# The first projection of two token blocks by seven quarter products, with sums kept in PSUM

## The chip, the cores and the metric

The kernel runs on one core of one Trainium2 chip. The core has TensorE (PE in the profile; its weight loads are shown apart as PEld), VectorE (DVE), ScalarE (ACT), GpSimd (POOL) and SyncE (SP), which issues most of the DMAs. The metric is the device time of one execution in microseconds (us). Three runs of the kernel before gave 297.3, 298.53 and 298.81 us; the median, 298.53 us, is the time before.

## The reference

```python
def _attn_ref(q, k, v):                      # 8 batches, 8 heads, 576 positions, 64 wide
    scores = scale * np.matmul(q, k.transpose(0, 1, 3, 2))
    gamma = 1.0 - 2.0 ** (-5.0 - np.arange(H, dtype=np.float32))
    Dmat = np.where(rel >= 0, gamma[:, None, None] ** rel[None, :, :], 0.0)
    return np.matmul(scores * Dmat[None, :, :, :], v)
...
def _moe_ref(x, w_in, w_out, alpha):         # x: 4608 x 512, w_in: 512 x 2048, w_out: 2048 x 512
    h = x @ w_in
    s = np.sin(alpha * h)
    g = h + s * s / (alpha + 1e-09)
    return (g @ w_out).astype(np.float32)
```

The output of the attention (a decayed, causal one without softmax) is the `x` of the second function. The first projection is `x @ w_in`, the second `g @ w_out`.

## The kernel before, in words

The 4608 tokens are worked on in nine blocks of 512. Blocks 0 to 7 are the first 512 positions of batches 0 to 7; block 8 holds the last 64 positions of all eight batches. A block goes through four steps.

1. **Attention** leaves the block's `x` transposed and in float16 (`xT`, `xS` for block 8): model dimension on the partitions, in four slices, tokens along the free dimension.
2. **First projection.** The 2048 columns of `w_in` are cut into 16 chunks of 128, numbered `fc`. `project n fc` makes one chunk of block n by four matmuls (one for each slice of the model dimension) that add up 128x512 float32 values in one bank of PSUM (`hps`, L1745).
3. **The activation.** For each chunk `sine` (ScalarE, L1753) reads the PSUM bank and writes `s`, `square` (mostly ScalarE, L1762) writes `ss`, and `product` (VectorE, L1769) reads `ss` and the bank and writes the chunk of `gT` in float16. With that the bank is free.
4. **Second projection.** For blocks 3 to 8 it is done by seven products of quarters in place of eight (the Strassen scheme in Winograd's form): the block's 512x2048 matrix `g` and the 2048x512 `w_out` are each cut into 2 x 2 quarters. `row_sum` (VectorE, L1832) makes the four sums S1 to S4 of quarters of `g`, half of each at a time; `weight_sum` made the sums T1 to T4 of `w_out` once. `part_product n i` (L1849) is product i, 16 matmuls of 256 columns, and `after_product` adds what it gives to kept results in SBUF (`low`, `mid`) or to an output tile `osb`, which a DMA then stores.

The eight banks of PSUM have fixed names: `m0` and `m1` are two banks each, `h0`, `h1`, `h2` and `op` one each. A step takes the bank that its line names, and waits until the bank's last reader is done. Each engine works through its own instructions in one fixed order; an instruction that waits holds up everything behind it on its engine.

That order is written out by hand: the string `TABLE` has one line for each step, and `run` issues the steps from top to bottom, so that the order of lines is the order on every engine. `A`, `V` and `G` in a line choose ScalarE, VectorE or GpSimd. The steps that the change and the prediction touch are `project`, `sine`, `square`, `product`, `row_sum`, `part_product` and `after_product`.

Of the kernel before, what the change touches and what calls it, by code (L numbers as in the profile page):

```python
# [929 lines left out]
at.to_state 7 2  # L930
at.masked 7 0 0 @ret0
sine 6 4 @s0
square 6 4 A @ss0
product 6 4
project 6 11 h2
square 6 2 A @ss3
product 6 2
# [2 lines left out]
project 6 5 h0  # L940
sine 6 5 @s2
square 6 5 A @ss1
at.scores 7 1 0 m0
at.scores 7 1 1 m1
# [1 line left out]
at.masked 7 1 0 @ret1
project 6 7 h1
part_product 5 6 op
load 7 k 2
cast 6 k 2 G  # L950
sine 6 7 @s2
# [31 lines left out]
part_product 5 5 op
after_product 5 5
at.values 7 0 False m0 relay=G
square 6 9 A @ss0
load 7 q 2
at.more 7 3 @s320
project 6 14 h2
sine 6 14 @s3  # L990
product 6 9
part_product 5 3 - first=5
product 6 10
square 6 14 A @ss2
product 6 14
sine 6 12 @s0
square 6 12 A @ss2
at.values 7 1 False m1 relay=G
after_product 5 3
at.values 7 0 True  # L1000
at.add_states 7 0
# [21 lines left out]
square 6 15 A @ss2
square 7 0 A @ss3
project 7 1 m0
project 7 3 h1
cast 4 q 2 G
cast 6 v 2 G
product 6 15
sine 7 1 @s3  # L1030
square 7 1 A @ss1
part_product 6 1 op
after_product 6 1
product 7 0
product 7 1
sine 7 3 @s0
square 7 3 A @ss3
row_sum 6 S2 1 V
project 7 2 h0
sine 7 2 @s3  # L1040
ends.scores 0 m0
ends.masked 0
crossed 4 2 q
# [987 lines left out]
```

## Time and profile before

| | before |
|---|---|
| median of three runs | 298.53 us |
| the profiled execution's own time | 297.56 us |
| its span, first to last instruction | 295.8 us |
| PE busy | 284.9 us, 96% of the span |
| DVE busy | 223.8 us, 76% |
| ACT busy | 218.1 us, 74% |
| POOL busy | 141.0 us, 48%; one instruction in the last 65 us |
| TensorE clock granted | 1.0 throughout |

The profiled execution took 297.56 us, 1.76 us more than its span and 0.97 us less than the median of the runs. Busy time of an engine is the union of its instructions' records. Records of neighbouring instructions on one engine overlap a little, so the time from one start to the next is the better price where instructions follow each other directly, and the record is the better price where another engine waits for the result.

### The profile page before, as it was taken

To read this page: it belongs to the slowest core of one execution; us is meant where nothing else is said; L and a number is where in the kernel's file an instruction comes from. 1 tells how busy PE (TensorE), PEld (TensorE's weight loads), DVE (VectorE), ACT (ScalarE), POOL (GpSimd) and SP (SyncE) were. 2 spreads that over 40 slices of the span, in tenths; PEclk is the share of its full clock that TensorE was granted. 3 is DMA by queue.
4 is the path that set the end of the run, shared out by engine and by line. 5 is a ranking of instruction groups with operands and counts; after the bars stand their busy time and mean duration, and the time that the engine had idled before them with its cause. 6 is when DMAs were issued, how large, how long until landed. Compare 5 with 4: busy or idle time off the path is not lost.

```text
span 295.8 us, 8407 instructions
## 1 busy us (share of the span) xinstructions
PE 284.9 (96%) x3480; PEld 182.6 (62%) x3480; DVE 223.8 (76%) x316; ACT 218.1 (74%) x361; POOL 141.0 (48%) x151
## 2 busy tenths in 40 slices
PE   6789999999999999999999999999999999999993
PEld 4566545555545544455666666666776677676883
DVE  2596977788349776889988798869868785877863
ACT  2578935997595897977878896798679878888500
POOL 5684678565688685736439933956232000000000
PEclk9999999999999999999999999999999999999999
DMA  7999999998998999978899985984423101200124
GB/s 216 347 234 210 243 282 320 253 256 217 244 225 184 174 164 229 250 148 204 164 239 163 251 180 145 232 151 120 88 77 104 38 2 38 73 15 23 53 73 124
DMA packets 121767, 49.95 MB, mean 169 GB/s; under 512 B 78721, under 2 KB 119681, under 8 KB 121729
## 3 DMA queue, kind: packets, MB, share of 16 engines
q1 hardware_dynamic: 117920, 44.78, 63.5%
q0 software_dynamic: 2688, 4.19, 7.8%
q8 instruction: 27, 0.44, 0.6%
q10 hardware_dynamic: 1120, 0.44, 0.6%
q14 instruction: 12, 0.09, 0.1%
HBM read 36.75 MB, written 9.44 MB: 156 GB/s over the span
## 4 chain that ended last, share of the span: by engine, by line
PE 82%; DMA 9%; DVE 3%; ACT 2%; POOL 1%; SPq 1%; issue 1%; ACTq 0%; POOLq 0%
PE hps L1745 40%; PE hps L1849 23%; PE ops L1785 12%; DMA raw<-in_v_dram 3%; DMA w_in<-in_moe_w_in_dram 3%; PE o L1606 3%; PE sc L1564 2%; DMA raw<-in_k_dram 2%; DVE S L1832 1%; PE kv L1506 1%; DVE gT L1769 1%; PE o L1628 1%; SPq L1350 1%; POOL k L1396 1%; ACT s L1753 1%
## 5 line engine op out<-in xcount | busy, mean ns | idle before, releaser
L1769 DVE SCALAR_TENSOR_TENSOR gT<-ss,inva,hps 128x512 f16<-128x512 f16 x144 | 103.7, 743 | 36.0 <-ACT ss L1762 32.5
L1745 PE MATMUL hps<-xT,w_in 128*128 128x512 f16 (+1 forms) x532 | 120.2, 372 | 0.6 <-DMA w_in<-in_moe_w_in_dram 0.6
L1753 ACT ACTIVATE s<-hps,alpha_t 128x512 f16<-128x512 f32 x144 | 96.1, 683 | 30.4 <-PE hps L1745 29.5
L1745 PEld LDWEIGHTS <-w_in 128*128 128x128 f16 x596 | 65.6, 114 | 51.4 <-DMA w_in<-in_moe_w_in_dram 0.9
L1762 ACT ACTIVATE ss<-s 128x512 f16<-128x512 f16 x125 | 76.9, 629 | 5.9 <-DVE gT L1769 3.3
L1785 PE MATMUL ops<-w_out,gT 128*128 128x512 f16 x192 | 46.0, 380 | 0.0
L1849 PEld LDWEIGHTS <-gT 128*128 128x128 f16 x384 | 37.3, 98 | 7.5
L1396 POOL TENSOR_TENSOR k<-raw,cn 128x1024 f16<-128x1024 f32 (+1 forms) x17 | 29.5, 1736 | 20.9 <-DMA raw<-in_k_dram 18.4
L1849 PEld LDWEIGHTS <-S 128*128 128x128 f16 x288 | 28.1, 98 | 6.1
L1785 PEld LDWEIGHTS <-gT 128*128 128x128 f16 x192 | 17.9, 98 | 20.3
L1396 POOL TENSOR_TENSOR q<-raw,cn 128x1024 f16<-128x1024 f32 x13 | 25.1, 1937 | 3.7 <-PE o L1606 2.4
L1849 PE MATMUL hps<-T,gT 128*128 128x256 f16 x192 | 22.8, 273 | 0.0
L1849 PE MATMUL hps<-w_out,S 128*128 128x256 f16 x192 | 22.8, 273 | 0.0
L1849 PE MATMUL hps<-w_out,gT 128*128 128x256 f16 x192 | 22.8, 273 | 0.0
L1551 POOL TENSOR_TENSOR s<-kvs,cn 128x256 f32<-128x256 f32 x21 | 13.8, 659 | 16.3 <-ACT kvs L1320 8.8
L1322 POOL CAST v<-raw 128x1024 f16<-128x1024 f32 x10 | 10.3, 1037 | 21.8 <-DMA raw<-in_v_dram 20.0
L1576 DVE TENSOR_TENSOR ret<-sc,mask 128x1024 f16<-128x1024 f32 x16 | 19.2, 1219 | 1.6 <-PE sc L1564 1.6
L1552 POOL TENSOR_TENSOR kvs<-s,kvs 128x256 f32<-128x256 f32 x21 | 17.5, 833 | 3.9 <-DVE kvs L1322 1.2
L1576 DVE TENSOR_TENSOR ret<-sc,mask_halved 128x768 f16<-128x768 f32 x16 | 15.1, 954 | 3.7 <-PE sc L1564 3.6
L1320 ACT CAST xT<-o 128x1024 f16<-128x1024 f32 (+1 forms) x15 | 16.2, 1122 | 1.9 <-PE o L1628 1.9
L1832 DVE TENSOR_TENSOR S<-gT,S 128x1024 f16<-128x1024 f16 x24 | 17.4, 730 | 0.1
L1745 PE MATMUL hps<-xS,w_in 128*128 128x512 f16 x64 | 14.8, 379 | 0.0
(78 smaller groups left out, 265.6 us busy)
## 6 DMA issues: line engine op xcount, KB each, us to landing
raw<-in_q_dram SPq DMA_DIRECT2D x16, 512.0 KB, 5.3
out_dram<-osb SPq DMA_DIRECT2D x32, 256.0 KB, 2.9
raw<-in_k_dram SPq DMA_DIRECT2D x8, 512.0 KB, 6.1
raw<-in_v_dram SPq DMA_DIRECT2D x8, 512.0 KB, 6.3
raw<-in_v_dram SPq DMA_DIRECT2D x32, 128.0 KB, 3.5
raw<-in_k_dram SPq DMA_DIRECT2D x32, 128.0 KB, 3.7
w_in<-in_moe_w_in_dram POOLq DMA_DIRECT2D x4, 512.0 KB, 11.9
w_out<-in_moe_w_out_dram POOLq DMA_DIRECT2D x4, 512.0 KB, 13.2
```

The source lines that it names most:

```text
L1320: eng.copy(d_, s_)
L1396: eng.tensor_tensor(dst[:, a0:a1].rearrange("p a r t d -> p t (a r) d"), t_.rearrange("p (t a) x -> p t a x", t=2)[:, :, a0:a1].rearrange( ...
L1551: nc.gpsimd.tensor_tensor(s32, self.kvs[:, c - 1], g1.unsqueeze(2).to_broadcast([P, 4, D]), MULT)
L1552: nc.gpsimd.tensor_tensor(self.kvs[:, c], s32, self.kvs[:, c], ADD)
L1576: nc.vector.tensor_tensor(ret.rearrange("p t (z x) -> p (t z) x", z=2)[:, :, 0:n], sc.rearrange("p t (z x) -> p (t z) x", z=2)[:, :, 0:n], ...
L1745: matmul(hps_of[n, fc][0][:, cols], w_in16[fc // 4][:, a, fc % 4 :: 4], xs[n][:, a, cols], start=(a == 0 and part != 1), stop=(a == KT - 1 ...
L1753: nc.scalar.activation(s_t, hps, mybir.ActivationFunctionType.Sin, bias=0.0, scale=alpha_t[:, fc : fc + 1],)
L1762: nc.scalar.activation(ss_t, s_t, mybir.ActivationFunctionType.Square)
L1769: nc.vector.scalar_tensor_tensor(gT[n][:, fc, :], ss_t, inva[:, fc : fc + 1], hps, MULT, ADD)
L1785: matmul(ops[n, c, cols.start][:, cols], gT[n][:, fk, c * P : (c + 1) * P], w_out16[:, fk, cols], start=(fk == 0), stop=(fk == FC - 1), sk ...
L1832: made = eng.tensor_tensor(out_, x, y, op)
L1849: matmul(acc[:, 256 * j : 256 * j + 256], lhs[:, x, 128 * j : 128 * j + 128], rhs[:, x], start=(tag is not None and j == js[0] and p == 0 ...
```

## The change

Blocks 7 and 8 now make their first projection by the seven-product scheme as well. Its left factor is `w_in` transposed, its right factor `xT`, and the quarters are halves of the model dimension by halves of the 2048 columns or of the 512 tokens.

- **Sums of the weights, once:** `in_sum` makes S1 to S4 of `w_in` in 16 instructions of 128x512 float16, 13 on GpSimd and 3 on VectorE. **Sums of x, for each of the two blocks:** four instructions `x_sum` of the same size, 4 on VectorE and 4 on GpSimd in all.
- **Pairs.** A pair u gives two chunks, and there are eight pairs to a block. Its four quarter results c11, c12, c21 and c22 and product 5 are 256 columns each; c11, product 5 and c12 lie in a two-bank buffer (`wide`, in `m0` or `m1`) and c21 and c22 in one bank (`narrow`, in `h0` or `h1`). Each product is two matmuls of 256 columns. The steps of a pair are, in the order that their data force: `pair` (products 1 and 5); `pair_copy` (c11 from PSUM to c21 in PSUM, ScalarE or VectorE) and `pair_keep` (product 5 to SBUF); `pair_6` (TensorE adds product 6 onto c21); `pair_add` (VectorE: c12 = c21 + product 5); `pair_7` (adds product 7 onto c21); `pair_end` (VectorE: c22 = c21 + product 5); `pair_3` onto c12, `pair_2` onto c11, and `pair_4` onto c21. Then one sine, one square and one product read the two halves in `wide`, and one of each read `narrow`. So `m0` with `h0` serves one pair at a time, `m1` with `h1` the next.
- **Where other work runs.** All lines of `TABLE` from the `square` of chunk 13 of block 5 on are written in a new order. From there on, 19 of the 32 `row_sum` steps are on GpSimd (before: none), eight of the 50 squares leave ScalarE (six to VectorE, two to GpSimd), two casts and one eviction change engine, two `to_state` steps go from GpSimd to VectorE. Steps before that line, the loads, and the number of second-projection products stay.

```diff
-project 8 2 h1
-project 8 1 h0
-sine 8 1 @s0
-square 8 1 A @ss1
-row_sum 7 S3 1 V
...
+pair 8 3 m0 h0
+part_product 7 2 - first=1
+sine 8 3 @s3
+pair_copy 8 3 A
+pair_keep 8 3 A @e1
+pair_6 8 3
+pair_add 8 3
+pair 8 2 m1 h1
+square 8 3 A @ss1
+product 8 3
+pair_copy 8 2 V
+pair_3 8 3
+pair_2 8 3
+sine 8 5 @s2
+row_sum 7 S2 1 G
+pair_7 8 3
+pair_end 8 3
+pair_6 8 2
+square 8 5 V @ss1
+pair_4 8 3
+pair_keep 8 2 A @e0
+sine 8 7 @s3
+square 8 7 G @ss2
+pair_add 8 2
+pair_7 8 2
+product 8 5
...
+    def in_product(n, u, i, dst, first=False):
+        g, x = divmod(u, 2)
+        left, right = FACTORS[i]
+        left = "S3" if i == 7 else left
+        lhs = in_piece(left, g)[..., x] if isinstance(left, str) else w_in_quarter(g, *left)[..., x]
+        rhs = x_piece(n, right) if isinstance(right, str) else x_quarter(n, *right)
+        for a in range(2):
+            matmul(
+                dst, lhs[:, a], rhs[:, a], start=(first and a == 0), stop=(a == 1), skip_group_check=True,
+            )
+
+    def pair(n, u, tag2, tag1):
...
+        both = psum.tile([P, 2, 512], F32, tag=tag2, bufs=1, name="wide")
+        one = psum.tile([P, 512], F32, tag=tag1, bufs=1, name="narrow")
+        pairs[n, u] = both[:, 0, 0:256], both[:, 0, 256:512], both[:, 1, 0:256], one[:, 0:256], one[:, 256:512]
...
+        in_product(n, u, 1, pairs[n, u][0], first=True)
+        in_product(n, u, 5, pairs[n, u][1])
+
+    def pair_copy(n, u, eng):
+        c11, p5, c12, c21, c22 = pairs[n, u]
+        copy(eng, c21, c11)
+
+    def pair_keep(n, u, eng):
...
+        copy(eng, kept_5[n, u], p5)
+
+    def pair_6(n, u):
+        in_product(n, u, 6, pairs[n, u][3])
+
+    def pair_add(n, u):
+        c11, p5, c12, c21, c22 = pairs[n, u]
+        nc.vector.tensor_tensor(c12, c21, kept_5[n, u], ADD)
+
+    def pair_7(n, u):
+        in_product(n, u, 7, pairs[n, u][3])
+
+    def pair_end(n, u):
+        c11, p5, c12, c21, c22 = pairs[n, u]
+        nc.vector.tensor_tensor(c22, c21, kept_5[n, u], ADD)
```

The order of instructions shows what this does to an engine. First VectorE in the first projection of block 8, in the kernel before. `gT<-ss,inva,hps` is `product`, `S..<-gT` and `gT<-gT` are `row_sum`, `mid` and `low` are `after_product`; numbers tell buffers apart.

```order
L1769 SCALAR_TENSOR_TENSOR gT_4598<-ss1_539,inva_69,hps_4612 128x512
L1769 SCALAR_TENSOR_TENSOR gT_4598<-ss3_563,inva_69,hps_4607 128x512
L1769 SCALAR_TENSOR_TENSOR gT_4598<-ss3_563,inva_69,hps_4651 128x512
L1769 SCALAR_TENSOR_TENSOR gT_4598<-ss1_539,inva_69,hps_4624 128x512
L1832 TENSOR_TENSOR gT_4598<-gT_4598 128x4x256
L1880 TENSOR_TENSOR mid_4695<-hps_4656,low_4673 128x512
```

Now the same engine in the same place of the changed kernel, from the `pair_add` of pair 8 1 to that of pair 8 3 (`wide_4700` with `narrow_4701` is pair 8 0, `wide_4735` with `narrow_4736` pair 8 1, the 478x buffers pair 8 3; `e0` and `e1` are kept products 5; L2021 is `pair_add`, L2028 `pair_end`, L1474 a copy, L1919 a square, L1924 `product`).

```order
L2021 TENSOR_TENSOR wide_4735<-narrow_4736,e1_4288 128x256
L2028 TENSOR_TENSOR narrow_4701<-narrow_4701,e0_4356 128x256
L2028 TENSOR_TENSOR narrow_4736<-narrow_4736,e1_4288 128x256
L1924 SCALAR_TENSOR_TENSOR gT_4699<-ss1_539,inva_69,wide_4700 128x512
L1919 TENSOR_TENSOR ss0_525<-s1_523 128x512
L1924 SCALAR_TENSOR_TENSOR gT_4699<-ss0_525,inva_69,narrow_4701 128x512
L1924 SCALAR_TENSOR_TENSOR gT_4699<-ss3_563,inva_69,wide_4735 128x512
L2163 TENSOR_TENSOR osb_4778<-hps_4591,mid_4491 128x512
L2021 TENSOR_TENSOR wide_4783<-narrow_4784,e1_4288 128x256
```

Between two products of a pair there now stand two adds, a square and an `after_product`, each of which waits for another engine.

GpSimd had one instruction left in this part of the kernel before (`sS<-kvs,cn`, the state of block 7). In the changed one it has these in the first projection of block 8 (`S..<-gT` and `gT<-gT` are `row_sum`, `in_T` is `x_sum`, `ss..<-s..` a square):

```order
L1978 TENSOR_TENSOR in_T3_4407<-in_T3_4407,xS_76 128x512
L1978 TENSOR_TENSOR in_T4_4730<-xS_76,in_T3_4407 128x512
L2100 TENSOR_TENSOR S2_0_2491<-gT_4278 128x1024
L2100 TENSOR_TENSOR gT_4278<-gT_4278 128x4x256
L2100 TENSOR_TENSOR S2_1_2582<-gT_4278 128x1024
L1919 TENSOR_TENSOR ss2_541<-s3_550 128x512
L1919 TENSOR_TENSOR ss1_539<-s0_517 128x512
L2100 TENSOR_TENSOR gT_4699<-gT_4699 128x4x256
```

Sums of the second projection that VectorE made before are behind each other on GpSimd, and two squares of block 8 are queued between them.

More of the change, by code (lines that the diff above doesn't have):

```diff
@@ L930 @@
[L930 to L937, printed above, removed]
+at.evict_bank 7 1 V
+part_product 4 4 h1
+row_sum 5 S1 0 V
+project 5 15 m0
+project 6 0 op
+sine 5 15 @s3
+square 5 15 A @ss3
+project 6 4 h0
+project 6 5 m1
+load 5 v 2
+after_product 4 4
+row_sum 5 S4 0 V
+sine 6 0 @s3
+product 5 15
+cast 4 v 2 A
+at.more 7 1 @s320
+square 6 0 V @ss3
+crossed 7 0 q @qT2
+at.more 7 2 @s320
+product 5 13
+part_product 5 1 h1
+project 6 2 h2
@@ L938 @@
+square 6 6 A @ss2
+project 6 8 h1
+sine 6 8 @s2
+square 6 8 A @ss0
+part_product 5 7 - first=6
+at.values 7 0 True
+at.add_states 7 0
+crossed 6 2 k
+product 6 7
+at.keep 7 0 A @xT0
+at.masked 7 1 0 @ret1
+product 6 6
+at.scores 7 1 1 m1
+project 6 10 h0
+sine 6 10 @s1
 load 6 v 2
 load 7 v 2
[L940 to L944, printed above, removed]
-at.masked 7 1 1 @ret3
[L946 to L951, printed above, removed]
@@ L983 @@
[L983 to L992, printed above, removed]
-product 6 10
[L994 to L1001, printed above, removed]
+cast 6 q 2 G
+product 6 8
+cast 6 v 2 A
+project 6 14 h1
+cast 4 q 2 G
+at.masked 7 1 1 @ret3
+in_sum S1 0 V
+crossed 4 2 q
+square 6 10 A @ss3
@@ L1023 @@
[L1023 to L1043, printed above, removed]
+product 6 14
+in_sum S2 1 G
+project 6 15 op
+project 6 13 h0
+project 6 9 h2
+ends.values 0 False m0
+crossed 6 2 q
+x_sum 7 T3 V
+x_sum 7 T1 V
 ends.scores 2 m1
@@ new lines @@
+product 7 1
+pair_copy 7 0 A
+in_sum S4 1 G
+pair_keep 7 0 A @e0
+pair_6 7 0
+pair_add 7 0
+pair_4 7 1
+sine 7 3 @s3
+row_sum 6 S2 0 G
+square 7 3 A @ss0
+part_product 5 3 - first=5
+row_sum 6 S2 1 G
+row_sum 6 S4 1 G
+in_sum S2 3 G
+in_sum S1 2 G
+in_sum S1 3 G
+after_product 5 4
+product 7 3
+pair 7 2 m0 h0
+pair_copy 7 2 A
+pair_7 7 0
+pair_end 7 0
+pair_3 7 0
+after_product 5 3
+x_sum 8 T3 G
+pair_2 7 0
+pair_6 7 2
+sine 7 0 @s2
+pair_keep 7 2 V @e0
+in_sum S4 2 G
+pair_add 7 2
+square 7 0 A @ss1
@@ new lines @@
+pair_4 7 0
+product 7 0
+sine 7 2 @s0
+square 7 2 A @ss0
+product 7 2
+part_product 6 6 h2
+pair_7 7 2
+pair_end 7 2
+pair_3 7 2
+pair_2 7 2
+row_sum 6 S4 0 V
+sine 7 4 @s2
+square 7 4 A @ss1
+pair 7 3 m1 h1
+part_product 6 1 op
+pair_copy 7 3 A
+pair_keep 7 3 A @e0
+pair_6 7 3
+pair_4 7 2
+product 7 4
+pair_add 7 3
+pair 7 4 m0 h0
+after_product 6 1
+after_product 6 6
+sine 7 6 @s2
+square 7 6 V @ss0
+product 7 6
+row_sum 6 S1 1 G
+pair_3 7 3
+pair_2 7 3
+sine 7 5 @s3
+square 7 5 A @ss1
+pair_7 7 3
@@ new lines @@
+pair_end 7 3
+part_product 6 2 - first=1
+pair_copy 7 4 A
+pair_keep 7 4 A @e1
+pair_6 7 4
+product 7 5
+pair_4 7 3
+pair_add 7 4
+sine 7 7 @s0
+square 7 7 A @ss0
+pair 7 5 m1 h1
+pair_7 7 4
+pair_end 7 4
+pair_3 7 4
+pair_2 7 4
+sine 7 8 @s1
+part_product 6 7 - first=6
+in_sum S4 3 G
+square 7 8 A @ss2
+product 7 7
+pair_copy 7 5 V
+pair_6 7 5
+pair_keep 7 5 A @e0
+product 7 8
+after_product 6 2
+row_sum 6 S1 0 G
+pair_4 7 4
+pair 7 7 m0 h0
+pair_add 7 5
+pair_3 7 5
+pair_2 7 5
+sine 7 10 @s1
```

595 lines of the change are left out of this document (351 added, 244 removed).

## The prediction

> **What bounds the kernel now.** I read the page first (busy shares, the chain that ended last), then the chain in order of time and a table by stage for the part that the change rewrites, then the groups by shape for prices and the timeline for hand-overs.
>
> ```profile
> PE 284.9 (96%) x3480; PEld 182.6 (62%) x3480; DVE 223.8 (76%) x316; ACT 218.1 (74%) x361; POOL 141.0 (48%) x151
> PE 82%; DMA 9%; DVE 3%; ACT 2%; POOL 1%; SPq 1%; issue 1%; ACTq 0%; POOLq 0%
> ```
>
> TensorE is busy for 96% of the span and makes up 82% of the chain. The rewritten part begins near 190 us; there the stages show
>
> ```profile
> 190.80:221.80 31.00, 31.00 (x485) 21.90 (x486) 24.18 (x35) 24.83 (x39) 13.67 (x15) 1.00 0.52 116
> 221.80:251.60 29.80, 29.70 (x373) 20.28 (x371) 22.46 (x33) 24.94 (x42) 2.76 (x4) 1.00 0.15 46
> 251.60:275.70 24.10, 24.10 (x160) 16.45 (x159) 18.54 (x28) 19.42 (x32) 0.00 (x0) 1.00 0.10 35
> 275.70:291.40 15.70, 15.68 (x144) 13.80 (x142) 11.63 (x19) 3.52 (x6) 0.00 (x0) 1.00 0.25 77
> ```
>
> (stretch, length, then busy us of PE, PEld, DVE, ACT, POOL). TensorE idles 0.11 us in 100.6, so every us of its work saved there is a us of time, and every wait added is one lost. The other engines have slack: VectorE is busy 18.5 of 24.1 us in the third stretch, GpSimd hardly at all. The chain gives TensorE's price per matmul:
>
> ```profile
> 249.62 3.49 PE hps L1849 x32
> ...
> 268.74 3.45 PE hps L1745 x16
> ...
> 275.66 15.73 PE hps L1849 x144
> 291.40 0.02 issue
> 291.42 0.42 DVE osb L1895
> ```
>
> A matmul of 512 columns takes 3.45/16 = 0.2156 us, one of 256 columns 3.49/32 = 0.1091 us. The last matmul is issued by 291.4; what follows (an add, a store) stays as it is.
>
> **What the change takes off TensorE.** Two blocks times 16 chunks times 4 = 128 matmuls of 512 columns go: 27.60 us. Two blocks times 8 pairs times 7 products times 2 = 224 of 256 columns come: 24.43 us. That is **-3.2 us**, the most the change can give; everything else can only cost. The prices of the rest:
>
> ```profile
> L1769 DVE SCALAR_TENSOR_TENSOR gT<-ss,inva,hps 128x512 f16<-128x512 f16 x144 | 103.7, 743 | 36.0 <-ACT ss L1762 32.5 <-POOL ss L1764 2.6
> L1753 ACT ACTIVATE s<-hps,alpha_t 128x512 f16<-128x512 f32 x144 | 96.1, 683 | 30.4 <-PE hps L1745 29.5
> L1762 ACT ACTIVATE ss<-s 128x512 f16<-128x512 f16 x125 | 76.9, 629 | 5.9 <-DVE gT L1769 3.3
> L1745 PEld LDWEIGHTS <-w_in 128*128 128x128 f16 x596 | 65.6, 114 | 51.4 <-DMA w_in<-in_moe_w_in_dram 0.9 <-issue 0.5
> L1849 PEld LDWEIGHTS <-gT 128*128 128x128 f16 x384 | 37.3, 98 | 7.5
> L1849 PE MATMUL hps<-w_out,S 128*128 128x256 f16 x192 | 22.8, 273 | 0.0
> L1895 DVE TENSOR_TENSOR osb<-hps,low 128x512 f32<-128x512 f32 x13 | 8.9, 686 | 2.9 <-PE hps L1849 2.8
> L1764 POOL TENSOR_TENSOR ss<-s 128x512 f16<-128x512 f16 x8 | 8.2, 1042 | 6.1 <-ACT s L1753 6.1
> L1764 DVE TENSOR_TENSOR ss<-s 128x512 f16<-128x512 f16 x11 | 6.0, 553 | 3.1 <-ACT s L1753 3.1
> L1320 ACT COPY kvs<-kv 128x256 f32<-128x256 f32 x4 | 1.5, 381 | 1.6 <-PE kv L1506 1.6
> L1895 DVE TENSOR_TENSOR osb<-hps,mid 128x256 f32<-128x256 f32 x2 | 0.8, 420 | 0.1
> L1745 PEld LDWEIGHTS <-w_in x596: 111/113/133, 21.2 to 275.1; 128*128 128x128 f16 x199
> ```
>
> No row shows an engine other than TensorE writing PSUM. The 32 adds and 16 copies into it I price like their nearest rows, which read PSUM and write SBUF: 0.42 us on VectorE, 0.38 on ScalarE. The low bound is the distance between neighbours rather than the record:
>
> ```profile
> 284.50 0.69 DVE L1880 TENSOR_TENSOR mid<-hps,low 128x512 f32<-128x512 f32 x1 [0.84 <-PE hps L1849]
> 285.11 0.68 DVE L1832 TENSOR_TENSOR S<-gT,S 128x1024 f16<-128x1024 f16 x1
> 285.71 0.68 DVE L1895 TENSOR_TENSOR osb<-hps,low 128x512 f32<-128x512 f32 x1
> 245.18 0.63 ACT L1762 ACTIVATE ss<-s 128x512 f16<-128x512 f16 x1
> 245.84 0.75 DVE L1769 SCALAR_TENSOR_TENSOR gT<-ss,inva,hps 128x512 f16<-128x512 f16 x1 [1.41 <-ACT ss L1762]
> ```
>
> Starts are 0.60 us apart where records are 0.69, so 0.09 less, 0.33; I take the record, since it is nearest where another engine waits, and keep 0.33 for the range. The high bound is a record stretched by GpSimd (+0.4, below). The square ends at 245.81 and its product starts at 245.84: a hand-over costs 0.03 us. By the Trainium skill (ScalarE: Activation LUTs, "Step-by-step: what each stage is for") ScalarE reaches PSUM with less latency than SBUF and VectorE is the one closer to SBUF. No run here shows it; by it the copies would cost less than 0.38 us and the adds perhaps more than 0.42, which partly cancels.
>
> A matmul of 256 columns is 0.273 us long by its record and the next starts after 0.109, so two of them occupy TensorE for 0.22 us and their sum can be read 0.19 us after that. The strided weight loads (113 ns, longest 133) lay under 216 ns of matmul; now they lie under 109. I take nothing for this (98 ns hide under 109) and keep 224 x 0.004 = 0.9 us for the range.
>
> **The waits that come.** A pair holds its buffers (`m0` with `h0`, or `m1` with `h1`) until its products have read them, so the pair after next waits. From the start of product 6 the chain to the free two-bank buffer is: product 6 0.22 + 0.19; add 0.42; products 3 and 2 0.44 + 0.19; sine 0.68; square 0.63; product 0.74; five hand-overs 0.15. Sum **3.66 us**. What TensorE can do meanwhile stands in its order. In the first three rounds of block 8 the one `part_product` of the round stands before product 6, and behind it come only steps of the two open pairs: in the first round 12 two-matmul steps, 2.6 us, in the next two 11, 2.4 us. The least wait is 1.0 + 1.25 + 1.25 = 3.5 us.
>
> With the queues the first round goes so, from the first matmul of pair 8 0: products 1 and 5, product 4 of pair 7 6, `part_product 6 3`, product 6 at 2.41 to 2.63. Its add is ready at 2.85 but stands behind two products of block 7 on VectorE: 3.07 to 3.49. Products 3 and 2 3.52 to 3.96. ScalarE's sine 4.20 to 4.88, square to 5.52. VectorE has two adds and two ends of the two pairs to do first (the last waits for product 7 of pair 8 1, issued only at 4.87 behind that pair's add, and ends at 5.73), so the product runs 5.64 to 6.38 and pair 8 3 starts at 6.44. TensorE's work in it is 5.05 us: a wait of 1.4. The same walk gives 1.4 for the round to pair 8 6 (the square of chunk 5 on VectorE stands between two adds there), 1.7 for that to pair 8 4, and 0.2 for the last, where three part products fill the chain. **Block 8: +4.7 us.**
>
> VectorE agrees: from pair 8 0 to the end of pair 8 5 it has 23 instructions of 256 elements (7.6 to 9.7 us), 15 products (0.65 apart to 0.74 long: 9.8 to 11.1), three squares (1.4 to 1.7) and four `after_product` (2.4 to 2.8), together 21.2 to 25.3 us against 24.7 us of TensorE work (24.43/2 + 0.2 + seven part products of 1.75). Before it had 18.5 in 24.1. An engine at 86 to 100% that also waits cannot keep TensorE running.
>
> In block 7 nearly every round has a part product inside the chain (2.4 + 1.75 = 4.2 us over 3.66), so waits are small: product 7 of the first pair behind its add 0.2, product 6 of pair 7 0 behind a copy 0.2, pair 7 7 behind a product of pair 7 4 0.3. **Block 7: +0.7.** Before it VectorE gets sums and squares but TensorE's banks are far enough ahead; the first pair waits for the last copy out of `m0`: **+0.5**. At the end `part_product 8 1` waits for the last product: **+0.2**.
>
> GpSimd takes 19 sums of 128x1024 (twice the 1.04 us row, 39.6 us), 17 of 128x512 (17.7) and two squares, 59 us beside the 16.4 it had. That is hidden by its idle time: each sum is due one to five part products (1.75 us each) later. Without that cover the last three (6.2 us in a row, against five part products, 8.7 us) would be late first.
>
> Sum: -3.2 + 4.7 + 0.7 + 0.5 + 0.2 = **+2.9 us**. The profiled execution's 297.56 us becomes 300.5; the median lies 0.97 higher, at 298.53, so I predict **301.4 us**.
>
> **Rivals.**
> 1. *The handed-over sums arrive early enough* (faster). Place: the chain of block 8. If an add or copy of 256 elements into PSUM were done after some 0.15 us instead of 0.42, the chain with its two adds before the product shrinks by 0.6 to 0.8 us a round, the other waits vanish and under 1.7 us of waiting remains: 295.3 (none) to 297.0. For it: TensorE never waited in this part before, with VectorE at 77%. Against: no record of 256 elements is under 0.38.
> 2. *Half of it* (no change): links 0.09 shorter and VectorE at its 21 us end. The chain becomes 3.3 us, waits 1.7 to 4.6 us in all: 297.0 to 300.0, around 298.5.
> 3. *VectorE and GpSimd get in each other's way* (slower still). Place: squares and sums with both inputs in SBUF.
>
> ```profile
> 195.32 0.68 DVE L1832 TENSOR_TENSOR gT<-gT 128x1024 f16<-128x1024 f16 x1
> 195.76 0.72 POOL L1551 TENSOR_TENSOR s<-kvs,cn 128x256 f32<-128x256 f32 x1 [2.70 <-ACT kvs L1320]
> 195.92 1.10 DVE L1832 TENSOR_TENSOR S<-gT 128x1024 f16<-128x1024 f16 x1
> ```
>
> The same sum takes 1.10 instead of 0.68 with GpSimd running, and GpSimd now runs to the end. Ten such instructions in the pair stages and the tail at +0.4 are 4 us, most on the chain: 303 to 306. The Trainium skill (SBUF — State Buffer, "Who interferes with whom") says the same: a VectorE instruction with two SBUF inputs contends with a GpSimd instruction that reads SBUF, one with a single SBUF input does not. The trace agrees with the first half (1.10 against 0.68); by the second the adds, which read PSUM and SBUF, stay at 0.42.
> 4. *The weight loads pace the products*, so that the change does not do what it says: at the longest load, 133 ns, 224 of them take 29.8 us, more than the 27.6 removed, and the time is about 307. Against it: the usual load is 113.
>
> **How the numbers follow.** Forecast 45% (300.0 to 303.5: waits of 4.7 to 8.2); rival 1 16%, rival 2 21%, rival 3 12%, rival 4 6%. One run of this kernel to the next can differ by about 0.5% (1.5 us), so that is the bound of "same". Faster: rival 1, 0.16. Same: rival 2, 0.21. Slower: 0.63. The range runs from 296.8, which leaves out most of rival 1's better half, to 305.0, which leaves out half of rivals 3 and 4.
>
> **What would show it.** In the profile after: TensorE no longer gapless between about 245 and 275 us, with waits of L1990 (the pairs' matmuls) on VectorE adding to 4 to 5 us, in the first three rounds of block 8; DVE above 90% there; 256-element adds near 420 ns. Adds well under 300 ns or a gapless TensorE would prove the forecast wrong; waits of L2117 on POOL would point to rival 3, matmuls of the pairs further apart than 0.11 us without a wait to rival 4.

## The result, and the profile after

The changed kernel is slower: 2.84% in the first timing (ratio to the kernel before 1.0284, 95% interval 1.0234 to 1.0333), and 306.64 us against 298.33 in a second set (1.0292, interval 1.0249 to 1.0334). That is some 8.4 us, where the forecast was 2.9. The direction was right, the size was not: the range ended at 305.0.

The profile that came with the first four runs is of a disturbed execution (311.89 us; the rewritten part begins 6 us late in it), as is that of `later_both8` below, so the profile shown here is one of the second set. Its page has, for the two lines that the prediction began with:

```profile
PE 287.1 (94%) x3576; PEld 191.8 (63%) x3576; DVE 236.1 (77%) x357; ACT 221.7 (72%) x374; POOL 199.3 (65%) x185
PE 57%; DMA 15%; POOL 8%; SPq 6%; DVE 5%; issue 4%; ACT 3%; POOLq 0%; DVEq 0%; ACTq 0%
```

TensorE is busy about as long as before (287.1 against 284.9 us), though it has 3.2 us less to do, and it now stands idle. Where, is read by stages. I count from the first matmul of `part_product 4 4`, which both kernels have at the same place (192.52 us before; in most profiles of this study it lies somewhere from 192.3 to 195.8, which is why lengths are compared and not moments). From there to the last matmul the kernel before takes 98.87 us. After, the same stretch in three stages: to the first pair, to the first pair of block 8, to the end (columns as in the prediction: busy us of PE, PEld, DVE, ACT, POOL, then the granted clock).

```profile
194.58:226.38 31.80, 28.99 (x498) 19.03 (x493) 28.94 (x44) 26.94 (x41) 21.09 (x20) 1.00 0.55 100
226.38:259.09 32.71, 32.28 (x279) 27.69 (x272) 26.21 (x49) 24.59 (x45) 30.01 (x19) 0.95 0.15 50
259.09:302.01 42.92, 39.20 (x340) 32.99 (x338) 33.27 (x62) 23.88 (x44) 23.31 (x12) 1.00 0.13 42
```

That is 107.43 us, 8.56 more, so the whole loss lies here. To see how much of each stage is work, one needs the same stages without pairs. The kernel `classic78` below has the new order with whole products:

```profile
193.56:225.14 31.58, 28.98 (x499) 19.03 (x493) 26.53 (x38) 26.95 (x41) 14.53 (x15) 1.00 0.54 99
225.14:257.14 32.00, 31.47 (x233) 22.90 (x226) 19.55 (x28) 22.37 (x37) 17.02 (x8) 1.00 0.15 51
257.14:295.57 38.43, 38.43 (x290) 29.01 (x288) 23.61 (x36) 19.10 (x31) 23.31 (x12) 1.00 0.15 46
```

TensorE's work there is 28.98 + 31.47 + 38.43 = 98.88 us, the 98.87 of the kernel before. With pairs a block has 8 x (8 x 0.2156 - 14 x 0.1091) = 1.58 us less, and product 4 of block 7's last pair (0.22) falls behind the second boundary: 28.98, 29.67 and 37.07 us. What a stage takes beyond that, I call lost. Two profiles of the change, this one and that of the first timing, give 2.8 and 2.5 us lost in the first stage, 3.0 and 3.1 in the second and 5.9 twice in the third, so a stage is good to some 0.3 us.

| stage | forecast | lost in the changed kernel |
| --- | --- | --- |
| before the first pair | 0.5 | 2.82 |
| block 7 | 0.7 | 3.04 |
| block 8 and the end | 4.9 | 5.85 |
| saved by TensorE | -3.2 | -3.16 |
| sum | +2.9 | +8.55 |

**Before the first pair.** The timeline of TensorE (start, length, engine, line, operands, count, and in brackets the idle time ahead and what ended it) and of the other engines there:

```profile
217.74 1.05 PE L1897 MATMUL hps<-xT,w_in 128*128 128x512 f16 x4
219.79 1.89 PE L1897 MATMUL hps<-xT,w_in 128*128 128x512 f16 x8 [1.00 <-DVE gT L1924]
...
223.55 0.32 PE L1845 MATMUL os<-rets,vs 64*64 64x64 f16 x16
225.45 0.32 PE L1845 MATMUL os<-rets,vs 64*64 64x64 f16 x16 [1.58 <-POOLq L1612]
...
227.01 3.41 PE L2117 MATMUL hps<-w_out,S 128*128 128x256 f16 x16
230.26 0.38 PE L1990 MATMUL narrow<-in_T,in_S 128*128 128x256 f16 x2
...
217.81 0.62 ACT L1472 CAST vs<-vs 128x512 f16<-128x512 f32 x1 [1.12 <-DMA vs<-in_v_dram]
218.99 0.75 DVE L1924 SCALAR_TENSOR_TENSOR gT<-ss,inva,hps 128x512 f16<-128x512 f16 x1 [1.51 <-ACT ss L1917]
224.68 0.68 DVE L2100 TENSOR_TENSOR S<-gT,S 128x1024 f16<-128x1024 f16 x1
225.53 0.61 POOL L1696 TENSOR_TENSOR sS<-kvs,cn 128x256 f16<-128x256 f32 x1 [2.17 <-DVE S L2100]
```

Two places of the order show. A projection waits 1.00 us for a product of block 6 whose square stands on ScalarE behind the cast of `vs`, and that cast waits 1.12 us for its transfer: the change had moved this cast (`cast 6 v 2`) from GpSimd to ScalarE. And the `os` matmuls wait 1.58 us for a mark on GpSimd's queue (L1612, an empty instruction by which GpSimd passes on that TensorE has finished a group). Ahead of it in that queue stands the mark of `row_sum 5 S4 1`, which waits for VectorE's sum at 224.68 to 225.36, and VectorE is busy for 28.94 of 31.80 us here.

Then 16 matmuls of 256 columns take 3.25 us (227.01 to 230.26) in place of 1.75. The granted clock (third column from the end) tells why:

```profile
224.00:226.00 2.00, 0.51 (x40) 0.40 (x40) 2.00 (x5) 1.54 (x3) 0.47 (x1) 1.00 0.00 0
226.00:228.00 2.00, 1.81 (x17) 1.39 (x18) 0.87 (x4) 1.50 (x4) 1.64 (x3) 0.67 0.00 0
228.00:230.00 2.00, 2.00 (x12) 1.39 (x11) 0.31 (x1) 1.72 (x3) 2.00 (x3) 0.50 0.00 0
230.00:232.00 2.00, 1.92 (x17) 1.63 (x16) 1.29 (x3) 0.00 (x0) 2.00 (x1) 0.98 0.00 0
```

After the stall the clock is halved for some 3.4 us (0.33, 0.50 and 0.02 of the clock are missing in the last three rows of 2 us each, together 1.7 us, which is 3.4 us at half clock), and these matmuls take 1.5 us longer. It falls into the second stage, so in this execution block 7's 3.04 us are this and 1.5 us of short waits.

**Block 7 at full clock.** The half clock is not why the change loses 3 us there. `no_square8` below leaves block 7 as the change has it, ran through it at full clock, and loses 3.1 us as well. There TensorE waits for a copy on ScalarE, the copy waits for a product on VectorE, and this product stands behind a sum that is held up (rows of VectorE, ScalarE, TensorE and GpSimd in turn):

```profile
228.19 2.50 DVE L2092 TENSOR_TENSOR gT<-gT 128x1024 f16<-128x1024 f16 x1
...
231.38 0.36 ACT L1464 COPY narrow<-wide 128x256 f32<-128x256 f32 x1 [1.62 <-DVE gT L1916]
...
231.79 0.38 PE L1982 MATMUL narrow<-in_T,in_S 128*128 128x256 f16 x2 [1.66 <-ACT narrow L1464]
...
228.03 2.12 POOL L2092 TENSOR_TENSOR S<-gT 128x1024 f16<-128x1024 f16 x1
```

The sum takes 2.50 us where GpSimd began one of its own 0.16 us earlier. The same sum takes 0.83 us in `again`, where TensorE at half clock let it start 1.84 us after GpSimd's, and 0.69 in `no_g`, where GpSimd makes none. The profile of the first timing, at full clock too, has the same sum of 2.50 us and a wait of 1.67. So the change loses 3 us in block 7 either way, to the half clock or to this wait.

**Block 8.** The waits of TensorE's matmuls from 258 to 290 us (us in total, times, longest), and the first round:

```profile
PE wide L1990 <- DVE wide L2021: 1.1, 4, 0.6
PE wide L1990 <- DVE gT L1924: 1.1, 2, 0.5
PE narrow L1990 <- DVE wide L2021: 0.7, 2, 0.4
PE narrow L1990 <- DVE narrow L2028: 0.5, 1, 0.5
PE narrow L1990 <- DVE narrow L1474: 0.4, 1, 0.4
```

```profile
261.93 0.38 PE L1990 MATMUL wide<-xS,in_S 128*128 128x256 f16 x2
262.47 0.38 PE L1990 MATMUL wide<-xS,in_S 128*128 128x256 f16 x2 [0.17 <-DVE wide L2021]
...
264.90 0.38 PE L1990 MATMUL narrow<-in_T,w_in 128*128 128x256 f16 x2
265.82 0.41 PE L1990 MATMUL wide<-xS,w_in 128*128 128x256 f16 x2 [0.54 <-DVE gT L1924]
```

These are the waits that the forecast named, on the engine that it named. But a wait costs more than its idle time: two matmuls take 0.22 us, the next start is 0.54 us later, and only 0.17 is counted as idle. The last matmul's record runs 0.16 us on after the next could have started, and that counts as busy. Ten waits with 3.71 us of idle time thus cost 5.3; four gaps of about 0.1 make up most of the rest.

### The profile page after: what moved, and what is told of

It is laid out like the page before. It is cut to its first block, busy times and chain, and to the rows that moved or that the text cites. A ratio compares the mean times of both kernels' runs of the same rounds, so it can differ in the third digit from the quotient of the medians.

```text
span 310.2 us, 8745 instructions
## 1 busy us (share of the span) xinstructions
PE 286.6 (92%) x3576; PEld 190.8 (62%) x3576; DVE 238.9 (77%) x357; ACT 222.1 (72%) x374; POOL 198.9 (64%) x185
## 4 chain that ended last, share of the span: by engine, by line
PE 64%; DMA 12%; DVE 8%; POOL 5%; ACT 4%; issue 3%; SPq 2%; DVEq 0%; ACTq 0%; POOLq 0%
PE hps L1897 24%; PE hps L2117 16%; PE ops L2053 12%; DMA raw<-in_v_dram 4%; PE wide L1990 4%; DVE gT L1924 3%; DMA raw<-in_k_dram 3%; DMA w_in<-in_moe_w_in_dram 3%; PE narrow L1990 3%; DMA qT<-q 2%; ACT s L1908 2%; PE o L1758 2%; PE sc L1716 2%; ACT ss L1917 1%; POOL k L1548 1%
## 5 line engine op out<-in xcount | busy, mean ns | idle before, releaser
L1897 PE MATMUL hps<-xT,w_in 128*128 128x512 f16 (+1 forms) x468 | 105.2, 371 | 1.0 <-DMA w_in<-in_moe_w_in_dram 0.5
L1924 DVE SCALAR_TENSOR_TENSOR gT<-ss,inva,hps 128x512 f16<-128x512 f16 x112 | 80.4, 742 | 23.3 <-ACT ss L1917 20.2
L1908 ACT ACTIVATE s<-hps,alpha_t 128x512 f16<-128x512 f32 x112 | 74.8, 683 | 23.5 <-PE hps L1897 22.1
L1897 PEld LDWEIGHTS <-w_in 128*128 128x128 f16 x468 | 51.3, 114 | 41.6 <-issue 1.5
L1917 ACT ACTIVATE ss<-s 128x512 f16<-128x512 f16 x117 | 72.5, 629 | 3.2 <-DVE gT L1924 0.5
L2053 PE MATMUL ops<-w_out,gT 128*128 128x512 f16 x192 | 47.5, 389 | 0.0
L1548 POOL TENSOR_TENSOR k<-raw,cn 128x1024 f16<-128x1024 f32 (+1 forms) x17 | 28.7, 1691 | 18.8 <-DMA raw<-in_k_dram 16.4
L2100 POOL TENSOR_TENSOR S<-gT,S 128x1024 f16<-128x1024 f16 x10 | 21.5, 2174 | 8.0 <-DVE S L2100 7.3
L1474 POOL CAST v<-raw 128x1024 f16<-128x1024 f32 x10 | 10.6, 1061 | 23.2 <-DMA raw<-in_v_dram 20.2
L1919 POOL TENSOR_TENSOR ss<-s 128x512 f16<-128x512 f16 x10 | 10.3, 1040 | 15.6 <-ACT s L1908 15.6
L1703 POOL TENSOR_TENSOR s<-kvs,cn 128x256 f32<-128x256 f32 x21 | 14.6, 693 | 8.1 <-ACT kvs L1472 7.7
```

Of the source, the lines that this page charges most:

```text
L1548: eng.tensor_tensor(dst[:, a0:a1].rearrange("p a r t d -> p t (a r) d"), t_.rearrange("p (t a) x -> p t a x", t=2)[:, :, a0:a1].rearrange( ...
L1897: matmul(hps_of[n, fc][0][:, cols], w_in16[fc // 4][:, a, fc % 4 :: 4], xs[n][:, a, cols], start=(a == 0 and part != 1), stop=(a == KT - 1 ...
L1908: nc.scalar.activation(as_halves(n, fc, s_t), hps, mybir.ActivationFunctionType.Sin, bias=0.0, scale=alpha_t[:, fc : fc + 1],)
L1917: nc.scalar.activation(ss_t, s_t, mybir.ActivationFunctionType.Square)
L1924: nc.vector.scalar_tensor_tensor(as_halves(n, fc, gT[n][:, fc, :]), as_halves(n, fc, ss_t), inva[:, fc : fc + 1], hps, MULT, ADD)
L2053: matmul(ops[n, c, cols.start][:, cols], gT[n][:, fk, c * P : (c + 1) * P], w_out16[:, fk, cols], start=(fk == 0), stop=(fk == FC - 1), sk ...
```

## The experiments

"Lost" is as above, by stage (before the first pair, block 7, block 8), against the TensorE work of the kernel's own products. Ratios are to the kernel before, with their 95% intervals.

| kernel | us | ratio | lost by stage |
| --- | --- | --- | --- |
| `again`: the change | 306.64 | 1.0292 (1.0249 to 1.0334) | 2.8, 3.0, 5.9 |
| `classic78` | 302.61 | 1.0160 (1.0130 to 1.0189) | 2.6, 0.5, 0.0 |
| `classic7` | 306.71 | 1.0285 (1.0228 to 1.0342) | 2.8, -0.2, 5.9 |
| `classic8` | 304.09 | 1.0189 (1.0153 to 1.0225) | 2.8, 4.0, 0.0 |
| `no_adds` | 301.75 | 1.0109 (1.0054 to 1.0164) | 3.0, 0.2, 3.1 |
| `no_g` | 304.63 | 1.0214 (1.0163 to 1.0264) | 2.7, 2.2, 5.7 |
| `no_adds_no_g` | 302.23 | 1.0138 (1.0085 to 1.0191) | 2.6, 0.2, 3.1 |
| `squares_A` | 306.69 | 1.0283 (1.0255 to 1.0310) | 2.7, 2.8, 7.1 |
| `later_both` | 305.62 | 1.0231 (1.0176 to 1.0285) | 0.8, 2.9, 5.9 |
| `later_mark` | 308.30 | 1.0304 (1.0230 to 1.0379) | 1.2, 3.0, 5.9 |
| `later_both78` | 299.34 | 1.0039 (1.0002 to 1.0075) | 0.9, 0.5, 0.0 |
| `later_both8` | 299.29 | 1.0019 (0.9986 to 1.0052) | not given |
| `later_no_g` | 303.23 | 1.0133 (1.0084 to 1.0181) | 1.0, 0.7, 5.7 |
| `later_row_v` | 305.08 | 1.0199 (1.0154 to 1.0243) | 1.0, 2.9, 5.9 |
| `later_both8_v` | 302.98 | 1.0130 (1.0092 to 1.0169) | 1.0, 3.4, 0.0 |
| `later_neither` | 299.72 | 1.0020 (0.9988 to 1.0053) | 1.1, 0.2, 3.0 |
| `no_square8` | 308.27 | 1.0324 (1.0280 to 1.0368) | 2.8, 3.1, 6.6 |
| `neither_square8` | 300.95 | 1.0063 (1.0028 to 1.0099) | 2.7, 0.2, 1.6 |

### The new order without pairs, and one block at a time

`again` is the change unedited. The others take whole products for one block or both, at the places of `pair` and `pair_6`; the steps between go from the order:

```diff
+        if n in (7, 8):                      # (7,) in classic7, (8,) in classic8
+            hps_of[n, fc] = [both[:, 0, :], None]
+            hps_of[n, fc + 2] = [one, None]
+            project(n, fc, None)             # and chunk fc + 2 in pair_6
+            return
```

`again`:

> The changed kernel once more, for a profile beside the other runs of this set. All theories: about 307 us, 8 above the kernel before. In the rewritten part (the first 193 us are the old work) the time lost to waits and restarts of TensorE should be some 11 us, against 6.1 in the forecast. Theory 1 (the forecast's: the chain of a pair and VectorE's queue) puts most of it in block 8; theory 2 (VectorE and GpSimd slow each other) shows VectorE sums well above 0.7 us beside GpSimd sums; theory 3 (each wait costs more than its idle time, since TensorE's first matmuls after it take longer) shows groups of matmuls after a wait taking 0.15 us longer than groups without one.

`classic78`:

> The new order of work, but the first projections of both blocks by whole products again (128 matmuls of 512 columns; no sums of quarters of w_in and x, no adds or copies into PSUM). GpSimd keeps the sums for the second projection that the change gave it. Theory 1 (the pairs' chain is the loss): TensorE has the 3.2 us of matmul back and no chain to wait for, 298 to 300 us. Theory 2 (GpSimd's sums slow VectorE, or are late themselves): 302 to 304, since 14 of the 19 sums of 1024 columns stay. A rival 4, the new order by itself is worse whatever the pairs do: 302 or more with waits of the second projection's products on POOL or on DVE.

`classic7`:

> Block 7 by whole products again, block 8 by pairs. The forecast's own sum for this: 298.5 - 1.6 + 4.7 + 0.2 = 301.8. If the loss lies as much in block 7 as in block 8 (contention and restarts in both): 302.5 to 304, half of the way back from 307 to 298.5.

`classic8`:

> Block 8 by whole products again, block 7 by pairs. The forecast's own sum for this: 298.5 - 1.6 + 0.7 + 0.5 = 298.1, no loss. If VectorE is full before the first pair and the sums for the pairs (quarters of w_in and x) cost there: 302 to 304, about half of the whole loss.

`classic78` measured 302.61 us, 4.3 above the kernel before, with no pair in it: not theory 1's 298 to 300, but what both others allowed. Its profile tells them apart. No product waits for a sum; TensorE idles 2.60 us ahead of block 7's first projection, at the same two places as above (0.79 and 1.58 us of it). So the order alone loses 3.1 us. `classic7` keeps all of block 8's loss, 5.9 us. Its time, 306.71 us, misses both expectations (301.8, and 302.5 to 304): its stages say that block 7 by pairs costs 3 us before what the pairs save, and the stretch is 1.6 us shorter than in `again` (105.82), but with runs from 304.6 to 308.4 us the median shows no gain. `classic8` measured 304.09, where the forecast's own sum was 298.1: without any chain in block 8, 6.8 us are still lost before and in block 7 (the half clock, which its profile has too, among them). The forecast was wrong about those two stages.

### The adds and GpSimd's sums

```diff
-pair_copy 7 1 A          # no_adds: all pair_copy, pair_keep, pair_add, pair_end
-pair_keep 7 1 V @e1
...
-in_sum S3 1 G            # no_g: in_sum, x_sum and (blocks 6 to 8) row_sum on G
...
-square 8 5 V @ss1        # squares_A: also 7 6, 7 12, 8 2 and, from G, 8 7, 8 4
+square 8 5 A @ss1
```

`no_adds`:

> Left out: the copies and adds of ScalarE and VectorE into PSUM (64 instructions of 256 columns and 32 copies of product 5), so the values of the pairs are not those of the reference; all seven products run, each starts its own part of the buffer. The sums of quarters on VectorE and GpSimd stay. Theory 1: all of the chain's waits go (4.7 + 0.7 us and the restarts with them): 299 to 301 from 307, or less. Theory 2 (contention and GpSimd's late sums): most of the loss stays, 303 to 305, with waits of the part products on POOL.

`no_g`:

> Left out: all sums that GpSimd makes from block 6 on (quarters of w_in, of x and of g); the products read an unsummed quarter in their place. Copies and adds into PSUM stay. Theory 2: VectorE runs undisturbed and no product waits for GpSimd: 302 to 304 from 307. Theory 1: within 1 us of the changed kernel, since GpSimd's work was hidden, and the chain of the pairs stays as it is.

`no_adds_no_g`:

> Left out: both, the copies and adds into PSUM and GpSimd's sums from block 6 on. If those two are the whole loss, what is left is the 3.2 us that TensorE saves: 295 to 296.5. Anything above 298 means a third cause in the new order itself (VectorE's queue before the first pair, restarts).

`squares_A`:

> The six squares of blocks 7 and 8 that VectorE or GpSimd make go to ScalarE (four from VectorE at 0.55 us, two from GpSimd at 1.04). Theory 1 with VectorE's queue as what the chain waits for: 0.5 to 1.5 us faster than the changed kernel. Theory 2: also faster, by the stretched squares (0.4 us each), 1 to 2 us. If ScalarE becomes the bound of a round: the same or slower by up to 1 us.

`no_adds` lies 4.9 us below the change (301.75 against 306.64, a little above the 299 to 301 of theory 1); by its stages 2.8 us of each block's loss go. It ran at full clock through block 7, and although VectorE's sum is held up there too (1.64 us), no copy is queued behind it. In block 8 the three waits that stay are all for the buffer that the product of the pair before last has to free:

```profile
262.42 0.38 PE L1926 MATMUL wide<-xS,w_in 128*128 128x256 f16 x2 [0.81 <-DVE gT L1860]
267.94 0.38 PE L1926 MATMUL wide<-xS,w_in 128*128 128x256 f16 x2 [0.78 <-DVE gT L1860]
273.81 0.38 PE L1926 MATMUL wide<-xS,w_in 128*128 128x256 f16 x2 [0.91 <-DVE gT L1860]
```

`no_adds_no_g` misses the 295 to 296.5 by six us: a third cause, the order, was there as its text allowed. `no_g` gains 2.0 us in time, less than theory 2 and more than theory 1 expected, and 1.1 in the stretch. Next to nothing of it is in block 8 (0.1 us), so contention with GpSimd (rival 3) is not what block 8 loses. In block 7 its 2.2 us lost include the half clock, so most of the rest is gone there. `squares_A` was expected to gain by the first two theories and gains nothing, as its third case allowed: its block 8 loses 7.1 us. ScalarE has no room in those rounds either, though it is busy only 23.88 of 42.92 us in the change.

### The two places of the order before the first pair

```diff
-cast 6 v 2 A             # later_both; not in later_mark
 ...
 square 6 14 A @ss0
+cast 6 v 2 A
 ...
-row_sum 5 S4 1 V told_to=G
 ...
 pair_6 7 1
+row_sum 5 S4 1 V told_to=G
```

`later_both`:

> The changed kernel with two steps put later, nothing left out: the sum row_sum 5 S4 1 with its mark for GpSimd goes from ahead of ends.values 2 to behind product 6 of the first pair, and ScalarE's cast 6 v 2 goes from ahead of two squares of block 6 to behind them. Theory (the time before the first pair is lost to these two places of the order: 1.58 us at the mark, some 1.0 us behind the cast): TensorE's idle time between the start of part_product 4 4 and the first pair falls from 2.8 us to about 0.3, the half clock after it goes too, and the time from 306.6 to 303 to 304.5 us. Rival (VectorE is full there, so something else of VectorE is late next): idle stays above 1.5 us and the time at 305.5 or more.

`later_mark`:

> Only the sum with its mark is put later. Theory: the wait of 1.58 us of the os matmuls on GpSimd's queue goes, the 1.0 us of a projection on a product of block 6 stays: idle of 1.0 to 1.3 us before the first pair, 304.5 to 305.5 us. Rival as above: 306 or more.

`later_both78` (with the edit of `classic78`):

> Both steps later, and both blocks by whole products: the new order alone, mended. Theory (the new order's whole price is those two places and 0.5 us in block 7): 298.5 to 300 us, from 302.6 without the mending. Rival (a third cause in the new order): above 301.

`later_both8` (with that of `classic8`):

> Both steps later, and block 8 by whole products as before, block 7 by pairs. By the sum of the pieces: TensorE 1.6 us less than before, about 0.3 us of idle ahead of the first pair, 1.3 to 1.6 us of short waits in block 7: 298.0 to 299.5, no difference from the kernel before that can be told. If pairs in block 7 pay once the order is mended: under 297.5.

Before the first pair 0.8 us stay lost instead of 2.8 (1.2 with the mark's step alone, where 1.0 to 1.3 of idle time was expected and 0.85 found). The new order with whole products comes to 299.34 us, from 302.61: its price was mostly these two places. That part of the theory stands. But the time of `later_both`, 305.62, misses the 303 to 304.5. The stretch is 2.1 us shorter (105.30) and not the 3.5 that the stall and the half clock seemed to cost together: block 7 loses as much as before. The time of `later_mark` (308.30, where 304.5 to 305.5 was expected) shows nothing, since its runs spread from 305.3 to 309.6 and its profile reaches the stretch only at 197.55 us; its stages say what the edit does. `later_both8` and `later_both78` are the best versions found, and neither beats the kernel before (ratios 1.0019 and 1.0039).

### Block 7: who is late

In `later_both` no stretch of half clock follows, and block 7 still loses 2.9 us. TensorE waits there for GpSimd (the waits from 223 to 256 us), and GpSimd is busy 23.84 of 24 us (last busy column of the window):

```profile
PEld L2117 <- POOL S L2100: 2.2, 2, 1.1
PE hps L2117 <- POOL S L2100: 1.6, 2, 0.8
```

```profile
232.00:256.00 24.00, 22.32 (x199) 19.26 (x197) 19.57 (x37) 18.20 (x33) 23.84 (x15) 1.00 0.15 51
```

In `again` these waits were not there: TensorE came 2.0 us later to the first pair and was at half clock after it, and the sums were in time. At full clock after the stall it waited behind VectorE's held-up sum instead, as shown above.

```diff
-row_sum 6 S2 0 G
+row_sum 6 S2 0 V
-row_sum 6 S2 1 G
+row_sum 6 S2 1 V
-row_sum 6 S1 0 G
+row_sum 6 S1 0 V
```

`later_no_g` (the edits of `later_both` and `no_g`):

> The two steps put later, and GpSimd's sums from block 6 on left out (the products read an unsummed quarter). If GpSimd's lateness is the larger part of block 7's loss: the time lost between the first pair and block 8's first falls from 2.9 us to 0.7 to 1.2 us, and the time from 305.6 to 303 to 304. If it is VectorE's queue: 2 us or more stay lost there, 305 or more.

`later_row_v` (`later_both` and the diff above):

> The two steps put later, and three sums of block 6's rows (S2 0, S2 1, S1 0: 2.1 us each on GpSimd) moved to VectorE (0.68 each); nothing left out. GpSimd's lateness as cause: the two waits on POOL in block 7 go (2.0 us with their starts), VectorE takes 2.0 us more of a stage in which it is busy 83%: 303.5 to 305. VectorE's queue as cause: 306 or more.

`later_both8_v` (`later_both8` and of the diff the row of S2 1):

> Block 7 by pairs, block 8 by whole products, both steps later, and the sum row_sum 6 S2 1 moved from GpSimd to VectorE; nothing left out. The wait of 0.98 us (with its start) on GpSimd in block 7 goes: about 1 us less in the rewritten part than with the sum on GpSimd (100.2 us), which is 0.3 us above the kernel before: 298.3 to 299.0 against 298.5 to 299, no difference. If VectorE is late instead: as with the sum on GpSimd, 299.3.

Without GpSimd's sums block 7 loses 0.7 us, the forecast's own figure, and TensorE is busy 30.18 of 30.35 us:

```profile
224.31:254.66 30.35, 30.18 (x279) 27.38 (x272) 26.51 (x51) 24.52 (x46) 0.00 (x0) 1.00 0.16 53
```

GpSimd's sums thus cost the mended kernel (`later_both`) 2.2 us (in the unmended one 0.9, by 3.0 against the 2.2 of `no_g`, both with the half clock). This price and that of the adds overlap and are not to be added up: leaving out either one, here or in `no_adds`, takes most of block 7's loss away. But the sums cannot simply go back. With three of them on VectorE the two waits on GpSimd go, TensorE waits 0.89 us for a copy and 1.06 for an add that stand behind VectorE's sums, and the loss is 2.9 as before. With one, `later_both8_v`, the kernel is 3.7 us slower than with it on GpSimd, where 298.3 to 299.3 us was expected. Its trace shows 1.5 us of this in the stretch (101.71 us against 100.19 for `later_both8`); where the rest comes from stays open. Its rows:

```profile
229.42 0.69 DVE L2040 TENSOR_TENSOR gT<-gT 128x1024 f16<-128x1024 f16 x1
...
229.46 1.67 POOL L1884 TENSOR_TENSOR in_S<-w_in,in_S 128x512 f16<-128x512 f16 x1
...
232.61 2.27 DVE L2040 TENSOR_TENSOR S<-gT 128x1024 f16<-128x1024 f16 x1
...
232.21 2.12 POOL L2040 TENSOR_TENSOR S<-gT 128x1024 f16<-128x1024 f16 x1
```

The first sum takes 0.69 us: it began 0.04 us before one of GpSimd's, and that one took 1.67 us where the next of its kind took 1.15. The second, of the same shape, takes 2.27 us: it began 0.40 us after GpSimd's. It does not merely slow down: it ends 0.55 us after GpSimd's, almost as if it had begun when that was done. The sums of 2.50 and 0.83 us above end 0.54 and 0.55 us after GpSimd's too. So in these rows the one that comes second waits. The Trainium skill (SBUF — State Buffer, "Who interferes with whom") says that a VectorE instruction with two SBUF inputs contends with a GpSimd instruction that reads SBUF, and calls this contention an exclusive lock. The trace agrees, with 2.27 us against 0.69.

### Block 8: adds or the chain to the buffer

```diff
-square 8 0 A @ss1        # no_square8: also 8 1, 8 4, 8 5, 8 8, 8 9, 8 12, 8 13
```

`later_neither` (`later_both`, `no_adds` and `no_g`):

> The two steps put later, GpSimd's sums and the copies and adds into PSUM left out. By the sum of the pieces: TensorE's 3.2 us less than before, 0.8 us before the first pair, 0.2 us in block 7, 3.1 us in block 8, where the pair after next still waits for sine, square and product: 0.9 us more than before, 299 to 300. Below 297.5 the chain without adds would not hold TensorE up.

`no_square8`:

> The changed kernel without eight squares of block 8, those of the chunks in the two-bank buffers (six on ScalarE, one each on VectorE and GpSimd): the product takes the sine itself. The chain as the bound of the rounds: 0.66 us less in each of three rounds, 5.8 us lost in block 8 become 3.7 to 4.2. VectorE's load as the bound: it loses only one square of 0.42 us, so 5.2 or more stay lost.

`neither_square8` (with the edit of `no_adds`):

> The changed kernel without the copies and adds into PSUM and without the eight squares of block 8's two-bank chunks. If the two follow one another in one chain (adds first, then sine, square, product): each round loses another 0.66 us, so the three waits of 0.97, 0.94 and 1.07 us on the product that stay without the adds become 0.3 to 0.4 each, and 1.0 to 1.3 us stay lost in block 8 instead of 3.1. If something else holds the buffers: 2.5 us or more.

`later_neither` gave 299.72 us and the expected stages: nothing else is left over. Note what that means: without a single add or GpSimd sum, and with 3.2 us less matmul, the kernel would be no faster than before, because 1.1 us ahead of the first pair and three waits of 1 us for the buffer stay.

`no_square8` was to lose 3.7 to 4.2 us in block 8 and loses 6.6. Part of that is the test's own doing: a sine's buffer is now held until its product, one sine waits 1.2 us for it, and with it one of TensorE's waits grows from 0.52 to 1.30 us. In the other two rounds 0.4 us and nothing were gained where 0.66 each was expected, and the last round, by two short waits, lost 0.4 more. So the squares are at most a small part of what the pairs wait for while the adds are there. With the adds gone, the squares count: 3.1 us lost become 1.6, not quite the 1.0 to 1.3 expected.

## Why the prediction was wrong

**Right:** the saving (-3.16 us by the counts); the prices of the new operations; the place of block 8's waits and nearly their size (5.85 us lost against 4.9); block 7's own waits (+0.7 against 0.68 once GpSimd is out); and no strided weight load paced a product, so rival 4 is out: where nothing waits, two products of two matmuls start 0.22 us apart. The groups with their means, for VectorE, ScalarE and GpSimd in turn, from 194.5 us on in `again`:

```profile
L2021 DVE TENSOR_TENSOR wide<-narrow,e 128x256 f32<-128x256 f32 x16 | 6.8, 428 | 4.3 <-PE narrow L1990 3.8 <-ACT e L1472 0.2
L2028 DVE TENSOR_TENSOR narrow<-narrow,e 128x256 f32<-128x256 f32 x16 | 6.8, 427 | 2.3 <-PE narrow L1990 2.0
...
L1472 ACT COPY narrow<-wide 128x256 f32<-128x256 f32 x10 | 3.7, 366 | 3.3 <-DVE narrow L2028 1.3 <-DVE gT L1924 1.1 <-PE wide L1990 0.9
...
L2100 POOL TENSOR_TENSOR S<-gT,S 128x1024 f16<-128x1024 f16 x10 | 21.5, 2179 | 8.0 <-DVE S L2100 7.3 <-PE hps L2117 0.8
L1952 POOL TENSOR_TENSOR in_S<-w_in,in_S 128x512 f16<-128x512 f16 x11 | 12.7, 1175 | 1.4 <-DVE in_S L1952 0.7 <-PE o L1758 0.7
```

An add into PSUM takes 428 ns (taken: 420), a copy 366 (380), a sum on GpSimd 2179 (2080) or 1175 (1040). Nothing here is far off, though the chain's 0.19 us from two matmuls to their reader is 0.03 more than its own rows give (0.273 + 0.109 - 0.218 = 0.16). What failed was where work was called hidden.

**Failed, first:** "before it VectorE gets sums and squares but TensorE's banks are far enough ahead; the first pair waits for the last copy out of `m0`: +0.5". It is 2.8, and it does not hang on that copy. The prediction's costing followed the pairs and never walked the 31.8 us ahead of them, where the diff moves a cast from one engine's queue to another's and a mark on GpSimd behind a VectorE sum.

**Failed, second:** "That is hidden by its idle time: each sum is due one to five part products (1.75 us each) later". GpSimd's 59 us were costed well and compared with its idle time over the whole stretch, and the forecast charged nothing for them. But they are bunched: in block 7 it is busy 30.01 of 32.71 us. So they are late, or they stand in VectorE's way. In the change at full clock a VectorE sum of 0.69 us takes 2.50 beside one of them and TensorE waits 1.66 us; in the mended order GpSimd has no pause from 232 to 256 us, and two part products come before their sums. Block 7 lost 3.0 us, against 0.7 in the forecast and in `later_no_g`.

**Not in the sum at all:** that a stall can be followed by a stretch of half clock. In `again` it made 1.5 of block 7's 3.0 us, but it added no time to the change, since at full clock block 7 lost as much.

**Off in size:** "Block 8: +4.7" and "+0.2" at the end. By rounds it lost 1.7, 2.1, 1.6 and 0.4 us against 1.4, 1.4, 1.7 and 0.2 forecast, and nothing at the end. The mechanism was partly another. The forecast had one chain per round from product 6 to the free buffer; in fact only 1.4 us are lost on the free buffer and some 3.9 on single adds, ends and copies inside the pairs, each with its 0.16 us. This fits `no_square8`, which shortens that chain and did not help. Also "DVE above 90% there" was wrong: from 261.49 to 280.90 us, in the first three rounds, VectorE is busy 15.46 of 19.41 us, 80%, so it was not full; TensorE, VectorE and ScalarE wait for one another in turn.

**Rival 3** had its mechanism right, and its place and size in part. A sum with both inputs in SBUF is held up, by up to 1.8 us (2.50 for 0.69) and not 0.4. In block 7 it holds up TensorE by 1.66 us in one place; in block 8 the adds read PSUM and stay at 428 ns, and there `no_g` gained 0.1 us. The forecast's sum had no term for it.

## What to carry to other kernels

Cost the stretch ahead of the new code as closely as the new code: each step that changes its engine or its place in an in-order queue, marks and casts that wait for transfers among them. Compare an engine's new work with its idle time in the window in which the results are due, not over the whole kernel, and ask which other engine is held up beside it. Where sums are handed around between three engines, count the hand-overs on TensorE: each wait costs its idle time and the tail of the matmul before it, and in block 8 they cost more than three times the 1.6 us that TensorE saved.
